# A decode-attention kernel: four heads per tile, 4 MiB loads into a shared ring, and scores summed by identity matmuls

## The chip, the cores and the metric

One core of a Trainium2 chip. The metric is device time in microseconds (us), lower is better. Each kernel ran several times; every run quoted here was in the normal (not slowed) state. The kernel before takes 1306.6 us (median of 4, 1305.9 to 1307.2).

## The reference

Softmax attention with one query per head: 8 x 32 = 256 heads, 4096 keys and values each, head size 128, all bfloat16. K and V together are 536.9 MB and every byte is used once, so the kernel is mostly a matter of loading.

```python
B, H, Sq, Skv, Dh = 8, 32, 1, 4096, 128
def reference(q, k, v):
    scale = q.shape[-1] ** -0.5
    scores = jnp.einsum('bhqd,bhkd->bhqk', q, k) * scale
    attn = _softmax(scores, axis=-1)
    return jnp.einsum('bhqk,bhkd->bhqd', attn, v)
```

## The kernel before

A head at a time: partition p holds 32 consecutive keys, so a load is 1 MiB with 8 KiB per partition. K has four buffers of its own, V eight. VectorE forms the product with the query and sums over d in a tree of halving adds; ScalarE does exp; TensorE does the weighted sum of V.

```python
kpool = ctx.enter_context(tc.tile_pool(name="kpool", bufs=4))
vpool = ctx.enter_context(tc.tile_pool(name="vpool", bufs=8))
# ... (cut)
    kv = k[b, h].rearrange("(p c) d -> p c d", c=C)          # C = 32
    kt = kpool.tile([P, C, D], BF16, name="kt", tag="kt")
    nc.sync.dma_start(kt[:], kv)
    nc.vector.tensor_tensor(out=prod[:, jj], in0=kt[:],
        in1=qb[:, h : h + 1, :].to_broadcast([P, C, D]), op=ALU.mult)
    # for each pair of heads: four halving adds, then a reduce
        for _ in range(4):
            half = width // 2
            nc.vector.tensor_tensor(out=rows[:, :, 0:half], in0=rows[:, :, 0:half],
                in1=rows[:, :, half:width], op=ALU.add)
            width = half
        nc.vector.tensor_reduce(out=st["scores"][:, gi0 : gi0 + npair, :],
            in_=rows[:, :, 0:width], axis=AX.X, op=ALU.add)
# ... (cut: maximum by GpSimd, exp on ScalarE, 8 matmuls per head for the values)
```

Instructions are traced in program order, but the framework's scheduler decides in which order they stand on each engine, and which semaphores they wait for. Both kernels leave that to it.

## Time and profile before

| | before |
|---|---|
| time | 1306.6 us |
| DMA engines busy | 99% (49.5% for each of the two load queues) |
| rate in full slices | 420 to 422 GB/s |
| VectorE (DVE) busy | 94% |
| TensorE (PE) busy | 56% |

The first lines are from the page of the kernel before. A digit is the busy share, in tenths, of one of 40 equal slices of the span (32.6 us each); the GB/s line is what the DMA engines moved in each.

```profile
DVE  7999999999999999999999999999999999999995
...
DMA  9999999999999999999999999999999999999993
GB/s 391 379 422 422 422 421 421 421 421 421 421 421 422 421 421 421 421 422 421 421 422 421 422 420 421 422 421 421 421 421 422 420 421 422 421 420 422 420 421 133
```

Two engines look full. Which one is the bound shows in the groups of instructions (busy us, mean ns of one | idle before it and what ended that):

```profile
L163 DVE TENSOR_TENSOR prod<-kt,qb 128x4096 bf16<-128x4096 bf16 x256 | 582.3, 2285 | 29.8 <-DMA kt<-in_k_dram 29.3
L175 DVE TENSOR_TENSOR prod<-prod 128x4096 bf16<-128x4096 bf16 (+4 forms) x516 | 568.8, 1143 | 0.0
```

VectorE's sparse waits for K, 29.8 us in all, and the flat 421 GB/s say that loads and VectorE are nearly level, with the loads the harder limit: 536.9 MB / 421.5 GB/s = 1274 us. The remaining 30 us are the slow start and the end.

### The profile page before, as it was taken

The numbers are of one execution on the slowest core, as the hardware profiler recorded it, in microseconds if no ns is written. First come the engines' busy times: TensorE is split into PE (matmuls) and PEld (weight loads), VectorE is DVE, ScalarE is ACT, GpSimd is POOL, SyncE is SP. The second block draws the span as 40 slices with busy tenths as digits, with TensorE's granted clock in tenths as the row PEclk, the third lists the DMA queues.
The fourth block names the chain that finished last, engine by engine and source line by source line (L and its number), as shares of the span: only waits on it lengthen the run. The fifth ranks groups of instructions, "written<-read, shape, count | busy, mean of one in ns | idle before, by whom it ended". The sixth has DMA issues, their size and how long they took to land.

```text
span 1304.4 us, 10166 instructions
## 1 busy us (share of the span) xinstructions
PE 725.8 (56%) x3204; PEld 298.3 (23%) x3268; DVE 1229.5 (94%) x1109; ACT 348.0 (27%) x1089; POOL 38.5 (3%) x78
## 2 busy tenths in 40 slices
PE   1466465465475564654655646556556456555466
PEld 0122122122122221221222212222222122222122
DVE  7999999999999999999999999999999999999995
ACT  1222222222232222232222322223222232222222
POOL 0200000000000000000000000000000000000000
PEclk9987787787777777877768778678677787777787
DMA  9999999999999999999999999999999999999993
GB/s 391 379 422 422 422 421 421 421 421 421 421 421 422 421 421 421 421 422 421 421 422 421 422 420 421 422 421 421 421 421 422 420 421 422 421 420 422 420 421 133
DMA packets 74107, 537.67 MB, mean 412 GB/s; under 512 B 8357, under 2 KB 8487, under 8 KB 8518
## 3 DMA queue, kind: packets, MB, share of 16 engines
q1 hardware_dynamic: 36864, 268.45, 49.5%
q10 hardware_dynamic: 36934, 268.52, 49.5%
q8 instruction: 25, 0.41, 0.1%
q14 instruction: 28, 0.23, 0.0%
q0 software_dynamic: 256, 0.07, 0.0%
HBM read 536.94 MB, written 0.07 MB: 412 GB/s over the span
## 4 chain that ended last, share of the span: by engine, by line
DMA 54%; DVE 41%; PE 3%; issue 1%; POOL 1%; ACT 0%; SPq 0%; ACTq 0%; POOLq 0%; DVEq 0%
DMA kt<-in_k_dram 54%; DVE prod L163 21%; DVE prod L175 17%; PE avp L242 3%; DVE scores L183 2%; POOL gmax L198 1%; ACT pw L211 0%; DVE negmax L202 0%; DVE rsum L224 0%; PE zp L220 0%; PE out L259 0%; DVE pmax L194 0%; SPq L156 0%; ACT stage L266 0%; POOL qrow L124 0%
## 5 line engine op out<-in xcount | busy, mean ns | idle before, releaser
L242 PE MATMUL avp<-vt,pw 128*128 128x512 bf16 x1984 | 604.9, 457 | 471.1 <-ACT pw L211 415.6
L163 DVE TENSOR_TENSOR prod<-kt,qb 128x4096 bf16<-128x4096 bf16 x256 | 582.3, 2285 | 29.8 <-DMA kt<-in_k_dram 29.3
L175 DVE TENSOR_TENSOR prod<-prod 128x4096 bf16<-128x4096 bf16 (+4 forms) x516 | 568.8, 1143 | 0.0
L242 PEld LDWEIGHTS <-pw 128*128 128x128 bf16 x2048 | 218.4, 117 | 771.4 <-ACT pw L211 496.8
L250 ACT ACTIVATE comb<-avp 128x512 bf16<-128x512 f32 x256 | 152.7, 597 | 377.9 <-PE avp L242 371.4
L211 ACT ACTIVATE pw<-scores,negmax 128x32 bf16<-128x32 f32 x256 | 86.7, 425 | 441.7 <-DVE negmax L202 441.7
L259 PE MATMUL out<-comb,masks 128*1 128x128 bf16 x1024 | 98.0, 218 | 22.4 <-ACT comb L250 19.7
L266 ACT ACTIVATE stage<-out,rsum 1x128 bf16<-1x128 f32 x256 | 89.3, 349 | 66.2 <-PE out L259 45.5
L183 DVE TENSOR_REDUCE scores<-prod 128x64 f32<-128x512 bf16 x129 | 86.8, 673 | 0.0
L259 PEld LDWEIGHTS <-masks 128*1 128x1 bf16 x1024 | 54.2, 82 | 111.6 <-issue 109.3
L130 PE MATMUL qp<-qrow,ones_row 1*128 1x512 bf16 x64 | 29.4, 460 | 82.2 <-ACT qb L137 42.4
L198 POOL PARTITION_ALL_REDUCE gmax<-pmax x66 | 34.2, 518 | 1149.2 <-DVE pmax L194 1149.2
L137 ACT ACTIVATE qb<-qp 128x512 bf16<-128x512 f32 x64 | 37.4, 584 | 66.6 <-DVE prod L163 19.4
L211 ACT ACTIVATION_READ_ACCUMULATOR pw<-scores,negmax 128x1 f32 x256 | 54.0, 211 | 0.0
L220 PEld LDWEIGHTS zp<-esum,ones_f 128*128 128x128 f32 x132 | 36.9, 315 | 39.4 <-ACT pw L211 29.6
L224 DVE RECIPROCAL rsum<-zp 128x4 f32<-128x4 f32 (+1 forms) x66 | 11.7, 178 | 24.4 <-PE zp L220 20.5
L220 PE MATMUL zp<-esum,ones_f 128*128 128x4 f32 (+2 forms) x132 | 34.0, 328 | 0.2 <-ACT pw L211 0.2
L130 PEld LDWEIGHTS <-ones_row 1*128 1x128 bf16 x64 | 5.9, 93 | 80.7 <-issue 39.3
L202 DVE TENSOR_SCALAR negmax<-gmax 128x4 f32<-128x4 f32 (+1 forms) x66 | 11.2, 170 | 9.1 <-POOL gmax L198 9.0
L194 DVE TENSOR_REDUCE pmax<-scores 128x4 f32<-128x128 f32 (+1 forms) x66 | 18.1, 275 | 0.0
L124 POOL DMA_DIRECT2D qrow<-in_q_dram x8 | 4.1, 518 | 102.7 <-PE qp L130 101.9
L111 DVE MEMSET pw<- 128x2048 uint32 x3 | 5.3, 1765 | 1.2 <-issue 1.2
(9 smaller groups left out, 2.3 us busy)
## 6 DMA issues: line engine op xcount, KB each, us to landing
vt<-in_v_dram ACTq DMA_DIRECT2D x256, 1024.0 KB, 16.5
kt<-in_k_dram SPq DMA_DIRECT2D x256, 1024.0 KB, 15.0
out_dram<-stage ACTq DMA_DIRECT2D x31, 2.0 KB
qrow<-in_q_dram POOLq DMA_DIRECT2D x8, 8.0 KB, 5.5
out_dram<-stage ACTq DMA_DIRECT2D x2, 0.2 KB
out_dram<-stage ACTq DMA_DIRECT2D x1, 1.0 KB
out_dram<-stage ACTq DMA_DIRECT2D x1, 0.5 KB
```

The costliest lines, as they stand in the source:

```text
L130: nc.tensor.matmul(qp[:], lhsT=ones_row[:], rhs=qrow_f[:, j * D : (j + QB_N) * D], start=True, stop=True,)
L137: nc.scalar.activation(out=qb_f[:, j * D : (j + QB_N) * D], in_=qp[:], func=ACT.Copy)
L163: nc.vector.tensor_tensor(out=prod[:, jj], in0=kt[:], in1=qb[:, h : h + 1, :].to_broadcast([P, C, D]), op=ALU.mult,)
L175: nc.vector.tensor_tensor(out=rows[:, :, 0:half], in0=rows[:, :, 0:half], in1=rows[:, :, half:width], op=ALU.add,)
L183: nc.vector.tensor_reduce(out=st["scores"][:, gi0 : gi0 + npair, :], in_=rows[:, :, 0:width], axis=AX.X, op=ALU.add,)
L198: nc.gpsimd.partition_all_reduce(gmax[:, 0:gsz], pmax[:, 0:gsz], channels=P, reduce_op=bass_isa.ReduceOp.max)
L211: nc.scalar.activation(out=st["pw"][:, gi, :, 0], in_=st["scores"][:, gi, :], func=ACT.Exp, bias=negmax[:, gi : gi + 1], scale=scale, accu ...
L220: nc.tensor.matmul(zp[:, 0:gsz], lhsT=ones_f[:], rhs=esum[:, 0:gsz], start=True, stop=True)
L242: nc.tensor.matmul(avp[:, :], lhsT=pw[:, gi, g8 * CB : (g8 + 1) * CB, :], rhs=vt[:, g8 * CB : (g8 + 1) * CB, :], start=(g8 == 0), stop=(g8 ...
L250: nc.scalar.activation(out=comb[:, :], in_=avp[:, :], func=ACT.Copy)
L259: nc.tensor.matmul(out2[0:1, :], lhsT=masks[:, m : m + 1], rhs=comb[:, m * D : (m + 1) * D], start=(m == 0), stop=(m == CB - 1),)
L266: nc.scalar.activation(out=stage[0:1, ot, :], in_=out2[0:1, :], func=ACT.Copy, scale=st["rsum"][0:1, gi : gi + 1],)
```

## The change

Its intent: loads with four times longer rows, to move the bytes faster, and much less VectorE work, so that nothing but the loads is left as a limit. Four heads form a tile: 32 partitions per head, 128 keys per partition, 32 KiB per partition, 4 MiB per load. The product is written in place over K; one add halves d from 128 to 64; then 16 matmuls with the identity sum the rest into PSUM, where one reduce finishes. K and V tiles share one ring of five slots.

```diff
-    kpool = ctx.enter_context(tc.tile_pool(name="kpool", bufs=4))
-    vpool = ctx.enter_context(tc.tile_pool(name="vpool", bufs=8))
+SLOTS = 5
+    kv_pool = ctx.enter_context(tc.tile_pool(name="kv_pool", bufs=SLOTS))
+    ps_s, ps_v, ps_o = (PSUM pools with bufs=2)  # shortened
+    ps_q, ps_z = (PSUM pools with bufs=1)        # shortened
 ... load (cut)
+        buf = kv_pool.tile([P, C, D], BF16, name=f"{kind}t", tag="kv")     # C = 128
+        (nc.sync if kind == "k" else nc.scalar).dma_start(...)
 ... scores_of(t) (cut)
+        for c0 in range(0, C, MC):                                          # MC = 64
+            part = kt[:, c0 : c0 + MC, :]
+            nc.vector.tensor_tensor(out=part, in0=part, in1=qb..., op=ALU.mult)
+            nc.vector.tensor_tensor(out=part[:, :, 0 : D // 2], in0=part[:, :, 0 : D // 2],
+                in1=part[:, :, D // 2 : D], op=ALU.add)
+        for u in range(NU):                                                 # NU = 1
+            for s in range(n):                                              # n = 16
+                nc.tensor.matmul(ps[:], lhsT=ident[:],
+                    rhs=kt[:, u * UC : (u + 1) * UC, s * DS : (s + 1) * DS], ...)
+            nc.vector.tensor_reduce(out=sc[:, u * UC : (u + 1) * UC], in_=ps[:], ...)
+        (pmax, spread, nmax, bias: small VectorE operations, one after the other)
+        (four exp on ScalarE, which also give esum)
+        zp = ps_z.tile([G, 1], F32, name="zp", tag="zp")
+        nc.tensor.matmul(zp[:], lhsT=esum[:], rhs=ones[:], start=True, stop=True)
+        rz = small.tile([G, 1], F32, name="rz", tag="rz")
+        nc.vector.reciprocal(out=rz[:], in_=zp[:])
 ... values_of(t): 32 matmuls av<-vt,w of 512 columns, copy, 4 small matmuls, scale by rz (cut)
+    for t in range(NT):
+        load("k", t + 1); load("v", t); ...; scores_of(t); values_of(t - 1)
```

## The prediction

> **What bounds it now.** The loads. The page's 40 slices show the DMA engines at 9 tenths or more in all but the last slice, at 420 to 422 GB/s from the third on; the view by stretches gives a DMA share of 1.01 and 421 GB/s at 300 to 400, 600 to 700 and 900 to 1000 us. K and V are 536.9 MB: 1274 us at 421.5 GB/s, of a 1304 us span. The other 30 us are edges: a start at 391 and 379 GB/s, and about 22 us after the last load. VectorE is busy 94% but waits only 29.8 us for K in all (groups by line): the close second, not the bound.
>
> **Costs per four heads (pace now 19.9 us).**
> - VectorE before: 1229.5/64 = 19.2 us. After: two products of twice the size (2 x 4.57 us), two adds of 2.28 us, a PSUM reduce (estimate 0.65 us), small operations (estimate 0.8 us): 15.1 us. Off the bound; it gives slack.
> - TensorE: 16 new identity matmuls of 512 columns beside 32 for the values; at the present mean busy of 0.305 us, 14.6 us. Copies, mask matmuls and GpSimd reductions get fewer: off the critical path.
> - DMA: same bytes, a quarter of the descriptors and semaphores. [...]
>
> **Critical path.** Only the 30 us from the DMA rate gain by themselves. What can be lost is feeding: K and V share 5 slots. K of tile t takes the slot of V of t-4, V of t that of K of t-1, and ScalarE issues V in order behind exponentials and copies. The built order puts one tile's small VectorE operations between the next tiles' products, so exp often waits for another K to land. Adding durations by hand over five tiles, the work alone needs some 85 us against 97 of DMA, with loads issued in bunches; the queues should hardly run dry, but slow TensorE bursts eat the margin. I allow 0 to 25 us of empty queues, 8 in the middle.
> Edges: 2 us before the first bytes, about 18 after the queues thin out (last K's products, scores, exp, 32 matmuls, output).
>
> **Predicted time:** 1244 + 2 + 8 + 18 = 1272 us; 8 times in 10 within 1254 to 1312. Faster by over 2%: 0.60; within 2%: 0.33; slower: 0.07.
>
> **What would show each step.** 429 to 433 GB/s in full slices. VectorE busy about 970 us (74 to 78%), PE 800 to 1000 us. Loads over 60% of the chain of waits. DMA slices under 9 tenths in the middle would be empty queues; SyncE's waits then name TensorE (values) as what frees slots.
>
> **What would make it wrong.** The rate staying at 421 [...]: about 1295. Identity matmuls slowed by reading four contiguous bf16 every 256 bytes, or TensorE at half clock: scores and values then reach the loads' pace and slots come free late: 1310 and more. VectorE stopping behind a reduce that waits for TensorE.

The sum came to 1244 + 2 + 8 + 18 = 1272 us. Its first term, all bytes at 431.5 GB/s, was the author's estimate. What was measured later: the changed kernel moved 425 to 438 GB/s in full slices, and the new form of the loads was worth 31.9 us (runs 5 and 6). The "quarter of the descriptors" shows in the pages as packets of K's queue: 36864 before, 9216 after. V's loads stand on ScalarE among its other work in the changed kernel's timeline: one is issued at 721.94, right behind a copy that waited 4.80 us for TensorE, another at 735.46 among the exponentials.

## The result, and the profile after

The changed kernel takes 1482.8 us (median of 4, 1479.6 to 1484.7): slower. Ratios here are of one kernel's fast runs to the other's in the same rounds, so not quite the ratio of the medians: 1.135, 95% interval 1.133 to 1.136.

The page after, the same lines:

```profile
DVE  4857567567467477477477477468468458558643
...
DMA  9978898798699599699699699699699599599692
GB/s 407 387 325 357 340 429 365 322 428 384 269 438 425 245 437 427 254 426 437 252 431 430 253 437 426 257 425 431 256 433 431 224 437 429 238 433 430 253 428 88
```

```profile
L132 DVE TENSOR_TENSOR kt<-kt,qb 128x8192 bf16<-128x8192 bf16 x128 | 564.2, 4417 | 382.5 <-DMA kt<-in_k_dram 382.5
L187 PE MATMUL av<-vt,w 128*16 128x512 bf16 x2048 | 535.8, 423 | 0.0
L144 PE MATMUL ps<-kt,ident 128*128 128x512 bf16 x1024 | 295.9, 444 | 319.4 <-DVE kt L135 319.4
```

Read the GB/s line first. Full slices do move 425 to 438 GB/s, more than the 421 of before, so the loads are faster when they run. But about every third slice falls to some 250. VectorE has indeed become much emptier (935 us busy against 1229.5), and waits 382.5 us for K where it waited 29.8. The loads are late, not slow.

Who keeps a load from starting shows in the waits of SyncE, which issues K's loads (us in total, times, longest):

```profile
SPq L106 <- PE av L187: 1293.3, 58, 47.3
```

SyncE stands for nearly the whole run waiting for TensorE's `av` matmuls, because K of tile t reuses the slot of V of tile t-4. That wait alone is no proof of a loss: run 4 below shows 901.7 us of it with full queues. What counts is whether other loads are still in flight meanwhile. The chain of waits also gives 61% to K's loads; that number looks like a loading-bound kernel, and alone would mislead.

The empty stretch is about 14 us long and comes once in five tiles. The timeline of the changed kernel around one (start us, us, engine, line, what; the idle time before it in brackets):

```profile
703.80 0.19 PE L175 MATMUL zp<-ones,esum 128*4 128x1 f32 x2
703.86 3.83 PE L187 MATMUL av<-vt,w 128*16 128x512 bf16 x17
707.21 8.76 DVE L132 TENSOR_TENSOR kt<-kt,qb 128x8192 bf16<-128x8192 bf16 x2 [8.37 <-DMA kt<-in_k_dram]
715.89 0.15 DVE L177 RECIPROCAL rz<-zp 4x1 f32<-4x1 f32 x1
...
716.18 0.19 PE L175 MATMUL zp<-ones,esum 128*4 128x1 f32 x2 [8.50 <-DVE rz L177]
716.24 5.13 PE L187 MATMUL av<-vt,w 128*16 128x512 bf16 x15
...
721.39 75.50 SPq L106 DMA_DIRECT2D kt<-in_k_dram  x5
```

and what ran in this stretch, and in the next two of its kind (busy us of each engine; the last columns are the granted clock, the DMA share and GB/s):

```profile
707.20:721.40 14.20, 5.70 (x21) 1.79 (x19) 13.28 (x6) 0.60 (x1) 0.00 (x0) 0.76 0.02 7
819.80:834.00 14.20, 5.79 (x21) 1.88 (x20) 13.28 (x6) 0.00 (x0) 0.00 (x0) 0.76 0.02 6
932.50:947.00 14.50, 5.93 (x22) 1.79 (x19) 13.28 (x6) 0.26 (x1) 0.00 (x0) 0.76 0.02 6
```

The DMA engines are 2% busy: no load at all is in flight. At 703.80 the sum of the exponentials, `zp`, of one tile (28) goes to PSUM, where this kernel's matmuls put their outputs, and 17 of its 32 value matmuls follow. Then TensorE comes to the `zp` of tile 29, which stands in the middle of those 32. There is one PSUM bank for all sums (`ps_z` has a single buffer), so it must wait until VectorE's reciprocal has read the sum of tile 28. On VectorE that reciprocal stands behind both products of tile 31, and these wait for K of tile 31, which lands only at 707.2. So TensorE idles 8.5 us, all of it after the last bytes in flight have landed; the other 15 value matmuls end at 721.4, and only then is V's slot free for the next load of K.

The built order on VectorE, as the scheduler left it (the number at the left is the place in the listing; kt_2705 is K of tile 31, rz_2576 and zp_2574 belong to tile 28, zp_2660 to tile 29):

```
299 L132 TensorTensor kt_2705<-kt_2705,qb_2363 128x8192 [waits DMAHW5_49,DMAHW0_49]
300 L132 TensorTensor kt_2705<-kt_2705,qb_2363 128x8192
301 L177 Reciprocal rz_2576<-zp_2574 4x1 [waits PE_49]
302 L135 TensorTensor kt_2705<-kt_2705 128x64x64 [waits DVE_49]
303 L177 Reciprocal rz_2662<-zp_2660 4x1 [waits PE_49]
```

and on TensorE, where the second sum stands between value matmuls of tile 28 and waits for VectorE:

```
3087 L187 Matmult av_2664<-vt_2535,w_2568 16x512
3088 L175 Matmult zp_2660<-ones_107,esum_2655 4x1 [waits DVE_49,Activation_49]
3090 L187 Matmult av_2664<-vt_2535,w_2568 16x512
```

VectorE kept this order in the trace: a reciprocal of 0.15 us, whose input was there at about 704, ran at 715.89, right after the products. TensorE's matmuls kept their order too: the 15 behind `zp` of tile 29 began at 716.24, after it.

Does this account for the loss? A period of five tiles is 112.6 us (721.4 to 834.0). Its 41.9 MB take 97.3 us at 431 GB/s (the rate of run 3 from 600 to 760 us), plus the 14.2 us stretch: 111.5 us, so about 1 us is left over. Over 64 tiles, 64/5 x 14.2 = 182 us, an estimate; the slow start, whose slices 3 to 5 are at 325 to 357 GB/s, and the 1 us per period come on top.

### The profile page after: what moved, and what is told of

Its sections match the earlier page's. It is cut to its first block, busy times and chain, and to the rows that moved or that the text cites. A ratio compares the mean times of both kernels' runs of the same rounds, so it can differ in the third digit from the quotient of the medians.

```text
span 1480.4 us, 8918 instructions
## 1 busy us (share of the span) xinstructions
PE 852.3 (58%) x3472; PEld 313.5 (21%) x3472; DVE 935.1 (63%) x642; ACT 177.4 (12%) x657; POOL 15.7 (1%) x36
## 3 DMA queue, kind: packets, MB, share of 16 engines
q1 hardware_dynamic: 9216, 268.44, 42.7%
## 4 chain that ended last, share of the span: by engine, by line
DMA 61%; PE 20%; DVE 16%; ACT 1%; issue 1%; ACTq 0%; DVEq 0%
DMA kt<-in_k_dram 61%; PE av L187 18%; DVE kt L132 15%; PE ps L144 1%; ACT w L170 1%; DVE kt L135 1%; PE zp L175 0%; ACTq L106 0%; DVE bias L164 0%; DVE rz L177 0%; PE op L195 0%; DVE sc L149 0%; ACT comb L192 0%; DVE pmax L153 0%; DVE spread L155 0%
## 5 line engine op out<-in xcount | busy, mean ns | idle before, releaser
L132 DVE TENSOR_TENSOR kt<-kt,qb 128x8192 bf16<-128x8192 bf16 x128 | 564.2, 4417 | 382.5 <-DMA kt<-in_k_dram 382.5
L187 PE MATMUL av<-vt,w 128*16 128x512 bf16 x2048 | 535.8, 423 | 0.0
L144 PE MATMUL ps<-kt,ident 128*128 128x512 bf16 x1024 | 295.9, 444 | 319.4 <-DVE kt L135 319.4
L135 DVE TENSOR_TENSOR kt<-kt 128x4096 bf16<-128x4096 bf16 x128 | 290.0, 2273 | 0.1
L187 PEld LDWEIGHTS <-w 128*16 128x16 bf16 x2048 | 191.4, 97 | 302.7 <-issue 116.2
L144 PEld LDWEIGHTS <-ident 128*128 128x128 bf16 x1024 | 104.4, 108 | 489.5 <-issue 413.2
L175 PE MATMUL zp<-ones,esum 128*4 128x1 f32 x128 | 12.2, 165 | 293.8 <-DVE rz L177 225.1
L170 ACT ACTIVATE w<-sc,bias 128x128 bf16<-128x128 f32 x256 | 113.0, 567 | 385.9 <-DVE bias L164 380.5
L149 DVE TENSOR_REDUCE sc<-ps 128x128 f32<-128x512 f32 x64 | 43.2, 675 | 139.2 <-PE ps L144 120.4
L192 ACT ACTIVATE comb<-av 16x512 bf16<-16x512 f32 x64 | 37.5, 586 | 585.6 <-PE av L187 585.6
L170 ACT ACTIVATION_READ_ACCUMULATOR w<-sc,bias 128x1 f32 x256 | 64.7, 253 | 0.0
```

Of the source, the lines that this page charges most:

```text
L132: nc.vector.tensor_tensor(out=part, in0=part, in1=qb[:, j : j + 1, :].to_broadcast([P, MC, D]), op=ALU.mult)
L135: nc.vector.tensor_tensor(out=part[:, :, 0 : D // 2], in0=part[:, :, 0 : D // 2], in1=part[:, :, D // 2 : D], op=ALU.add,)
L144: nc.tensor.matmul(ps[:], lhsT=ident[:], rhs=kt[:, u * UC : (u + 1) * UC, s * DS : (s + 1) * DS], start=(s == 0), stop=(s == n - 1),)
L149: nc.vector.tensor_reduce(out=sc[:, u * UC : (u + 1) * UC], in_=ps[:], axis=AX.X, op=ALU.add)
L170: nc.scalar.activation(out=w[:, :, g], in_=sc[:], func=ACT.Exp, bias=bias[:, g : g + 1], scale=scale, accum_out=esum[:, g : g + 1],)
L175: nc.tensor.matmul(zp[:], lhsT=esum[:], rhs=ones[:], start=True, stop=True)
```

## The experiments

Theory A is the one just told: operations of an earlier tile, small but needed to free V's slot, stand in the built order of VectorE and TensorE, which both kept, behind the product of a K that has not landed, and the shared ring ties the next K to that slot. A second kind of this stop is the `bias`, which exp needs. Rival B: TensorE, with 50% more matmuls of 512 columns, is too slow. Rival C: five slots of 4 MiB are too few or too coarse. Rival D: the long loads themselves get in each other's way. Runs 1 to 4, 5 to 8, and 9 and 10 each shared a chip and the runs of the kernel before (about 1306.5 us in each). All results were correct but those of the two kernels that only load.

### Run 1: two banks for the sums

```diff
-ps_o = (... name="ps_o", bufs=2 ...)
+ps_o = (... name="ps_o", bufs=1 ...)
-ps_z = (... name="ps_z", bufs=1 ...)
+ps_z = (... name="ps_z", bufs=2 ...)
```

The order built on ScalarE and SyncE stays the same, on VectorE almost; on TensorE 37 of 3409 matmuls move, most of them the sums themselves, a few places forward. The same work stands on every engine.

> Edit: two PSUM banks for the sums zp (one for the output products), the built order is nearly unchanged. Theory A (a freed slot waits for V's matmuls, and these stop at a zp matmul that waits for a reciprocal standing behind the product of a K that has not landed): one of the two kinds of stop is gone, the other (the bias behind such a product) stays; 1340 to 1440 us, TensorE's waits for the reciprocal gone. Rival B (TensorE is too slow or cold) and rival C (five slots of 4 MiB are too few): within 1% of 1480 us.

Measured: 1363.7 us, ratio to before 1.044 (1.042 to 1.045). From its timeline, the same place as above:

```profile
660.85 0.19 PE L175 MATMUL zp<-ones,esum 128*4 128x1 f32 x2
660.90 5.34 PE L187 MATMUL av<-vt,w 128*16 128x512 bf16 x24
662.49 8.76 DVE L132 TENSOR_TENSOR kt<-kt,qb 128x8192 bf16<-128x8192 bf16 x2 [8.33 <-DMA kt<-in_k_dram]
...
666.28 29.12 SPq L106 DMA_DIRECT2D kt<-in_k_dram  x3
```

The second `zp` no longer waits, and the next load of K is issued 3.8 us after K landed instead of 14.2 us. One PSUM bank is worth 119 us (1482.8 - 1363.7). Rivals B, C and D, which this edit does not touch, cannot explain that. The other kind of stop remains, as expected: every third slice is still at 362 to 375 GB/s. The chain of waits of this run shows one such delay (start us, us, what):

```profile
587.51 36.27 DMA kt<-in_k_dram
...
623.80 4.43 DVE kt L132
628.23 0.15 DVE bias L164
...
630.45 8.63 PE av L187 x32
639.08 0.02 issue
639.09 23.30 DMA kt<-in_k_dram
```

A `bias` runs right behind a product whose K has only just landed; then come exp and 32 value matmuls, and 15.3 us after K landed the next K starts. How much of the dips this kind makes by itself no run separates; run 2, which puts the biases first, removes them.

### Run 2: no product of the next tile before this tile's bias

```diff
+    last_bias = [None]
+    def after_bias(ins):          # an edge of order alone, no semaphore
+        if last_bias[0] is not None:
+            tc.add_manual_dep(ins.ins, last_bias[0].ins.name, (NoSync), ...)
-            nc.vector.tensor_tensor(out=part, ..., op=ALU.mult)
+            after_bias(nc.vector.tensor_tensor(out=part, ..., op=ALU.mult))
-        nc.vector.tensor_scalar(out=bias[:], ...)
+        last_bias[0] = nc.vector.tensor_scalar(out=bias[:], ...)
```

> Edit: one ordering edge, no product of the next tile before the bias of this one on VectorE; same work, same five slots. Theory A: both kinds of stop are gone (the reciprocal then stands behind the next tile's adds at most, never behind a product two tiles on); VectorE pays a wait of some 4 us per tile for the scores, about 19 us per tile, so 1260 to 1320 us and full DMA slices throughout. Rival B and C: VectorE loses overlap and nothing is gained; 1480 us or more.

Measured: 1338.6 us, ratio 1.025 (1.023 to 1.026). Much faster than 1482.8, as Theory A says and B and C do not, but outside my range of 1260 to 1320. The empty stretches are gone (every slice but the last two is at 9 tenths), yet the GB/s line reads 402 to 424 in most slices:

```profile
GB/s 407 424 438 424 436 422 416 406 409 416 398 409 415 408 421 406 407 421 403 417 410 405 417 404 405 421 402 404 420 405 414 407 408 419 404 407 419 403 369 32
```

Its chain of waits says why; one tile of it (start us, us, what):

```profile
687.73 0.70 DVE sc L158
...
689.44 8.76 DVE kt L141 x2
698.19 4.41 DVE kt L144 x2
702.60 0.07 DVE rz L186
702.67 5.52 PE ps L153 x16
```

VectorE and TensorE now take turns: 20.48 us from one tile to the next (687.71 to 708.19, where the 16 matmuls end), above the 19.5 us that its loads need at 431 GB/s. I had put 4 us for the wait for the scores; it is 5.5 us. These matmuls begin after 7.1 us of idle TensorE; their weight loads come every 0.43 us for the first 3.8 us, and the next six within 1.23 us. In the changed kernel the same 16 took 3.63 us right behind other matmuls, at a granted clock of 1.00. There, too, matmuls were slower after idle time: behind the 8.5 us of idle TensorE in the stretch above, the granted clock was 0.50 from 716.2 to 719.8 us and 1.00 from there to 721.4.

### Run 3: the same five slots, three for K and two for V

```diff
-kv_pool = ctx.enter_context(tc.tile_pool(name="kv_pool", bufs=SLOTS))
+k_pool = ctx.enter_context(tc.tile_pool(name="k_pool", bufs=3))
+v_pool = ctx.enter_context(tc.tile_pool(name="v_pool", bufs=2))
-        buf = kv_pool.tile(...)
+        buf = (k_pool if kind == "k" else v_pool).tile(...)
```

> Edit: the same five slots of 4 MiB, split into three for K alone and two for V alone, so that K no longer waits for V's slot. The scheduler's order still puts biases behind later products. Theory A says that the loop runs K, product, exp, V's matmuls, V's slot, K; cut between the last two, K is prefetched again: 1250 to 1340 us. Rival C (capacity): 1440 us or more, V starved with two slots.

Measured: 1284.2 us, ratio 0.983 (0.982 to 0.984). The same bytes of buffer, no edge of order and still one PSUM bank for the sums, and 199 us less: capacity is not the cause. In the built order, biases still stand behind later products; from 600 to 760 us the loads nevertheless run at 431 GB/s with a DMA share of 1.00. The reason is that K's loads no longer wait for V's matmuls. SyncE's longest entry is now that for VectorE's work on an earlier K, and no entry names `av`:

```profile
SPq L107 <- DVE kt L136: 682.4, 55, 34.3
```

The scheduler built a different order here, in which `zp` waits for the reciprocal 39.9 us in all, where it waited 225.1 us in the changed kernel. So this run alone does not separate slots from order. Run 1 helps: without any such wait of `zp`, but with the ring as it was, it still took 1363.7 us.

### Run 4: run 2, with the scores in two halves

```diff
-    UC = 128
+    UC = 64
```

On top of run 2's edge, this makes two groups of 8 identity matmuls with a reduce each.

> Edit: the ordering edge of the second run, and the scores in two halves of 64 positions, so that VectorE waits for 8 identity matmuls instead of 16. Theory A: VectorE's work with its wait is some 17 us per tile, below the 19.2 us that 8.39 MB take at 437 GB/s; DMA-bound, 1245 to 1275 us, faster than the kernel before by 3 to 5%. Rivals B and C: not faster than 1480 us by more than a few per cent.

Measured: 1274.8 us, ratio 0.976 (0.974 to 0.978): faster than both kernels. That is at the upper edge of the range I gave, and 2.4% where I expected 3 to 5%. Its page:

```profile
DMA  9999999999999999999999999999999999999993
GB/s 401 436 431 426 428 431 433 434 431 427 429 432 430 434 429 431 430 431 432 431 434 428 430 429 432 433 429 431 430 431 431 430 433 430 431 428 432 433 429 120
```

This is the profile that I had predicted for the change itself: about 431 GB/s throughout, though with some 25 us after the loads thin out where I had put 18. TensorE's busy time (876 us) is even higher than after the change (852 us), which rules out rival B as the bound. The five shared slots are the same, so rival C falls too. The chain of waits gives only 19% to loads here and 49% to VectorE, which waits 18.4 us for K in all: VectorE's chain is nearly level with the loads. Runs 8 and 9 test which of the two is the bound.

### Runs 5 and 6: the loads alone

Two kernels without arithmetic (one VectorE copy of one element per partition from each tile): 4 MiB loads with 32 KiB per partition in five slots, and 1 MiB loads with 8 KiB per partition in twelve.

> Only the loads of the changed kernel (32 KiB per partition, 4 MiB each, five slots, K from SyncE and V from ScalarE), no arithmetic, so a wrong result on purpose. [...] 429 to 438 GB/s in full slices, 1235 to 1265 us in all. If the loads themselves were slow or got in each other's way (rival D): clearly above 1274 us.

> Only loads, in the form of the kernel before (8 KiB per partition, 1 MiB each, twelve slots); wrong result on purpose. [...] 421 to 422 GB/s as in the kernel before, 1275 to 1285 us, and the difference to the run with 32 KiB is 25 to 40 us. If the rate of before was set by VectorE's pace after all, it is faster than that.

Measured: 1252.3 us and 1284.2 us. The GB/s lines, 32 KiB first:

```profile
GB/s 402 436 436 429 427 436 436 429 427 436 436 429 427 435 436 430 427 435 436 430 428 434 435 430 430 431 435 432 429 432 435 432 429 432 435 432 430 431 435 358
```

```profile
GB/s 390 422 422 422 421 422 422 422 422 422 422 422 422 422 422 421 422 422 422 423 422 422 422 422 422 422 422 422 422 422 422 422 422 421 422 421 422 422 422 331
```

The form of the loads is worth 31.9 us by itself; the forecast had 1274 - 1244 = 30, from the estimate of the rate. Rival D falls. Row length, size of the load and bytes of buffer were changed together here. Run 8 rules out the buffer; which of the other two pays is not separated. The kernel before was bound by the second of these lines: its full slices show the same 421 to 422 GB/s.

### Run 7: six slots

```diff
-SLOTS = 5
+SLOTS = 6
-o_pool = (... name="o_pool", bufs=2)
+o_pool = (... name="o_pool", bufs=1)     # makes room
```

> Edit: six slots in place of five (one output stage to make room); with an even number K's slot comes from the K three tiles before and V's from V, so the ring no longer ties K to V's matmuls. Biases still stand behind products in the built order. Theory A: 1255 to 1310 us, as with the split pool. Rival C (capacity alone): one slot more gives a part of the loss back, 1380 to 1440 us.

Measured: 1272.9 us, ratio 0.974 (0.973 to 0.976), all middle slices between 429 and 433 GB/s. With an even number of slots and K and V allocated in turn, a K always takes the slot of an earlier K. A sixth slot recovers 210 us where run 3 recovers 199 with five, so what matters is less the capacity than whose slot it is. The scheduler's order changed here too: `zp` waits for the reciprocal only 25.4 us. But exp waits 671.9 us for `bias`, where it waited 380.5 us in the changed kernel; that stop is still there and no longer reaches the loads.

### Run 8: run 4 with the loads in the old form

```diff
-        cuts = [C]
+        cuts = [C // 4] * 4
```

Every load becomes four of 8 KiB per partition.

> Edit: the fourth run with every load cut into four of 8 KiB per partition (1 MiB each); order and slots the same. If the fourth run is bound by the loads, the cut costs what the row size costs: 421 GB/s in full slices and 1295 to 1310 us, level with the kernel before. If it is bound by VectorE's chain, no change from 1275 us.

Measured: 1303.3 us, ratio 0.998 (0.996 to 0.999), at 420 to 422 GB/s in full slices:

```profile
GB/s 391 421 422 420 421 421 421 420 421 422 420 421 421 421 421 421 422 420 421 422 420 421 422 420 421 421 421 421 420 422 421 420 422 421 421 421 422 421 422 151
```

So run 4 is bound by its loads, and its 28.5 us over this run (1303.3 - 1274.8) are the loads' form. With the old loads, all of the rest of the change (VectorE busy 77%) is worth 0.2% against the kernel before.

### Runs 9 and 10: less VectorE chain, and one more slot

Run 9 adds to run 4 an edge that puts the first half's add before the second half's product, so that half of the identity matmuls run under VectorE's work. Run 10 adds six slots to that.

> Edit to the fourth run: a second ordering edge, the first half's add before the second half's product, so that 8 of the 16 identity matmuls run under VectorE's later work. It shortens VectorE's chain by some 2 us per tile. If the fourth run is bound by the loads in every full slice, that buys nothing there and at most a few us after the last load: 1266 to 1276 us. If VectorE's chain set the pace, some 2 us x 64 would come off, down to the 1252 us of the loads alone.

> The ninth run with six slots (one output stage): the loads run further ahead. Bound by the loads already, so the same within 0.5%: 1264 to 1276 us.

Measured: 1277.6 and 1279.9 us, ratios 0.978 (0.977 to 0.979) and 0.980 (0.978 to 0.981). Both lie a little above my ranges, run 10 by 4 us. Nothing is gained, as a kernel bound by its loads should show: from 40 to 80 us and from 1180 to 1220 us runs 4, 9 and 10 all move 430 to 432 GB/s. In the profiles of runs 4 and 10 the last bytes land near 1250 us, so the 4.5 us by which run 10's span is longer (1277.6 against 1273.1) lie behind the loads. Why run 9 is 2.8 us slower than run 4, on another chip, stays open.

## Why the prediction was wrong

- **What bounds the kernel before: right.** The loads alone in the old form need 1284 us and show the same 422 GB/s.
- **The rate of the new loads: right.** 431.5 GB/s was the estimate; run 4 shows 426 to 436 in full slices, and the two kernels that only load differ by 31.9 us where 30 were predicted. Why the new loads are faster is not shown: size and row length changed together.
- **VectorE and TensorE: right.** 935 us busy against "about 970", 852 us in "800 to 1000". Per piece on VectorE: a product 4.42 us against 4.57, an add 2.27 against 2.28, a reduce 0.68 against 0.65, the small operations 1.1 us per tile against 0.8.
- **Feeding: wrong, and this is the step that failed.** The prediction said "the queues should hardly run dry" and allowed "0 to 25 us of empty queues, 8 in the middle". The queues ran dry for 14.2 us in every five tiles, some 182 us in all by the estimate above. Against run 4, which has the same loads and nearly the same arithmetic, the changed kernel loses 208 us (1482.8 - 1274.8), not 8.
- **What the hand addition left out.** It counted durations over five tiles ("the work alone needs some 85 us against 97 of DMA") and did see exp waiting behind a later K. It didn't carry the wait of one `zp` for the reciprocal of the sum before, through the single PSUM bank. That wait closes a loop: K lands, products (8.8 us), reciprocal, `zp`, the rest of V's matmuls (5.1 us), V's slot, the next K. None of it overlaps with a load once the other slots are filled. Run 1 cuts this link alone and gains 119 us. Run 2 also moves the biases forward, and removes every empty stretch. Run 3 cuts the loop at the slot, with a changed order, and recovers 199 us.
- **Two warnings in the prediction came true in form.** It named empty slices with SyncE waiting for the value matmuls, and slots that come free late. But it gave the cause as slow matmuls. The identity matmuls are not slow: 16 took 3.63 us, 227 ns each, with an operand of four contiguous bf16 every 256 bytes, against 221 ns for value matmuls on contiguous ones (30 in 6.64 us). The other suspect, half clock ("cold" in the expectation of run 1), has a small part: after TensorE's idle 8.5 us, with a granted clock of 0.50 for the first 3.6 us, the 15 value matmuls took 5.13 us, and at 221 ns they would have taken 3.3, so about 1.8 of the 14.2 us (an estimate from these numbers).
- **The sign of the idea was right.** With one ordering edge and one constant changed (run 4), or with one more slot (run 7), the change is 2.4 to 2.6% faster than the kernel before, near the 1272 us that I predicted for it. That nearness is in part luck: run 4 has no empty queues where I allowed 8 us, and an end of 25 us where I had 18.

## What to carry to other kernels

When two streams share a ring of buffers, work out whose slot each load takes, and follow the whole loop from a load's landing to the next load's start, through every wait in the built order of every engine, including small operations and PSUM tiles with a single buffer; the sum of durations per engine (85 us against 97 here) did not show this loop. The loads headed the chain of waits here (61%), while the GB/s line dipped to some 250 in about every third slice: the loads started late. Where a profile looks like that, ask the issuing queue whom it waits for while nothing is in flight. Give K and V slots of their own, or keep what frees a buffer ahead of work that waits for the next load: here either was enough (runs 3 and 7, and run 4).
